# Linear attention and two feed-forward layers: the prices of the list schedule are changed

## The chip, the cores and the metric

The kernel runs on one core of a Trainium2 chip. The metric is the device time of one execution in microseconds (us). Three executions of the kernel before took 1591.6, 1592.91 and 1593.28 us; their median is 1592.91 us.

## What is computed

Inputs are q, k and v (8 batches, 8 heads, 576 positions, 64 values a head). Three steps follow each other, all in float32:

```python
kv = einsum('bhsd,bhse->bhde', k, v)             # attention without a softmax
out = einsum('bhsd,bhde->bhse', q, kv)
x = out / sqrt(mean(out*out) + 1e-6) * g_norm    # reordered to 4608 tokens x 512
x = (s * relu(x @ w_in1)**2 + b) @ w_out1        # 512 -> 2048 -> 512
h = x @ w_in2
y = (h * sigmoid(h)) @ w_out2                    # 512 -> 2048 -> 512
```

## The kernel before

The 4608 tokens are nine blocks of 512. TensorE multiplies in a 32-bit format with fewer mantissa bits, so each factor is held as a rounded part and a rest (`rnd` on ScalarE, line 214, and `rest` on VectorE or GpSimd, line 217), and one exact product is three matmuls of 512 columns: high by high, high by low, low by high (`mm3`, line 209). The kernel is bound by these.

The work has these stages.

1. **Attention of block 0**, in four pairs of heads (`attention_pair`, line 437, with `normalize`, line 565). A pair takes k, v and q from DRAM, multiplies k by v (`kv`, line 488: twenty small matmuls), copies that out of the bank (`kv_out`), turns q by a transposition on VectorE (`q_turn`, line 509), multiplies q by kv (`o`, line 518), multiplies the left-over 64 positions (`rem`, line 522, tile `r_ps`) and stores those (`orem`). While TensorE has nothing to do here, small warm-up matmuls fill it (line 1244).
2. **Seven plain blocks of layer 1** (`unit`, line 698). A unit is one block by 128 of the 2048 hidden columns: four exact products into bank `h` (`mm1`), then on ScalarE the relu, the square and the affine step (lines 730 to 737), the rounding (`g_hi`) and the rest (`g_lo`), and four exact products into the four banks `acc` (`mm2`). Sixteen units make a block. Beside the first block the weights of layer 1 are put together from a packed form (`decode`, line 275): load, three operations on ScalarE, three on VectorE and one on GpSimd for each weight tile. Four tiles come last, since room for them has to be made first (`turn`, line 1193): once all other tiles are done, the four come in halves through two load buffers `raw2`. Among them is the tile `wi15`, which unit 15 needs. Attention of the blocks 1 to 7 runs beside the units, and so does the making of factors for the next stage.
3. **Five stages on pairs of blocks** (`hidden`, line 923, and `outputs`, line 1060), one of layer 1 and four of layer 2, in which a two by two split of the matrices takes seven products for eight. Their results pass through three banks X, Y and Z and tiles `tmp`; ScalarE applies the curve (`curve`, `square`, `affine`, lines 997 to 1005).
4. **The last block of layer 2** as plain units again.

No engine's instruction order is written out by hand. Each operation is handed to a `Plan` (line 20) with the engine or engines that can do it and a price in us, a key (roughly the unit at which it is due), what it needs, what it makes, and which buffers it takes and gives back. `Plan.run` (line 45) walks a clock of its own: on each engine it looks for the operations that could start soonest by the prices so far, takes among those within 0.02 us the one with the lowest key, and emits it. So a price never changes an instruction; it changes when the planner believes things to be over, and with this in which order instructions stand in the queues of TensorE, ScalarE, VectorE, GpSimd and SyncE (which issues the loads and stores), and for some copies and rests which engine does them. Once emitted, each queue runs in its order. Warm-up matmuls carry the highest key and the limit `until=40`: the planner drops those that would begin after 40 us of its own clock.

The prices that matter here are those of the products (lines 543, 555, 720, 777, 954 and 1088), of the affine steps (lines 743 and 1012), and two functions of a width n for ScalarE, which give 0.525 and 0.622 us at 512 columns:

```python
    def act2(n):
        return {ACT: 0.11 + n * 1.0e-3}

    def act(n):
        return {ACT: 0.1 + n * 0.83e-3}
```

Of the kernel before, what the change touches and what calls it, by code (L numbers as in the profile page):

```python
# [19 lines left out]
class Plan:  # L20
# [19 lines left out]
    def add(self, engines, key, fn, needs=(), makes=(), takes=(), gives=(), move=None, opens=(), until=None):  # L40
        self.ops.append((key, len(self.ops), engines, fn, needs, makes, takes, gives, move, opens, until))
        for b in gives:
            self.users[b] = self.users.get(b, 0) + 1
# [89 lines left out]
def kernel(  # L133
# [30 lines left out]
    T = NCH * P  # L164
# [3 lines left out]
    LAG2 = 1.6  # L168
# [13 lines left out]
    def layer_of(tp):  # L182
        return 0 if tp < NL1 else 1
# [12 lines left out]
    tp = ctx.enter_context(tc.tile_pool(name="tp", bufs=1))  # L196
# [54 lines left out]
# [5 lines that stand above are left out]
# [181 lines left out]
    def attention_pair(bb, p, key, before=None):  # L437
# [99 lines left out]
        for i in range(P // Q):  # L537
# [2 lines left out]
        fr = (0, 0) if z else me  # L540

        prev, prev_r = ([], []) if z else ([("x32",) + before], [("ro",) + before])
        add({"PE": 0.8}, key, kv, needs=[f("k"), f("v"), ("kr",) + fr, ("vr",) + fr] + prev_r, makes=[f("kv")],
            takes=[b["psk"]], gives=[b["kv"], ("wo12", 0) if z else b["rem"]])
        add({ACT: 0.21, DVE: 0.26}, key + 0.3, kv_out, needs=[f("kv")] + ([("kvf0L",)] if z else []), makes=[f("kvf")],
            takes=[b["kvf"]], gives=[b["psk"]])
# [5 lines left out]
        add(act(T), key + 0.4, q_hi, needs=[f("qT")], makes=[f("qh")], takes=[b["qs"]], gives=[b["qT"]])  # L552
        add(both(T), key + 0.5, lambda e: rest(e, st["ql"], st["qT"][:, :T], st["qh"]), needs=[f("qh")], makes=[f("ql")],
            gives=[b["qT"]])
        add({"PE": 0.65}, key + 1.5, o, needs=[f("kvl"), f("ql"), f("kvh"), f("qh")] + prev,
            makes=[f("o")], takes=[b["pso"]], gives=[b["kvs"], b["qs"]])
        add({"PE": 0.2}, key + 2.2, rem, needs=[f("kvf"), f("qT")], makes=[f("r")], takes=[b["psr"]],
            gives=[b["kvf"], b["qT"]])
# [139 lines left out]
    def unit(u):  # L698
        layer, t, m = units[u]
        lb = LASTU if layer else t  # L700
        def ready(kind):
            if layer == 1:
                return [("w", 1, kind, m)]
            return [("w", 0, kind, m, c) for c in range(2 if (kind, m) in late else 1)]

        def w_gives(kind):
            if layer:
                return [("win" if kind == "i" else "wout", ("last", m))]
            return lent_to[f"w{kind}{m}"] if t == TP - 1 else []

        def mm1(kk):
            def go(e):
                if kk == 0:
                    h_t[u] = psum(("h", u), "h")
                w, f_ = w_t["i", layer, m], slice(kk * P, (kk + 1) * P)
                mm3(h_t[u], w[:, 0, f_], w[:, 1, f_], *xs[lb, kk], kk == 0, kk == KD - 1)
            return go

        for kk in range(KD):
            add({"PE": 0.648}, u + kk * 0.02, mm1(kk),  # L720
                needs=[("x", lb, kk)] + ready("i") + [("mm1o", u, kk - 1)] * (kk > 0) + ([("mm1o", u - 1, kk)] if u - 1 in units else []),
                makes=[("mm1", u, kk)], opens=[("mm1o", u, kk)], takes=[("h", u)] * (kk == 0),
                gives=([xs_of(lb, kk)] if lb != TP - 1 else [("ya", f"xh{kk}"), ("ya", f"xl{kk}")]) * (m == KF - 1) + w_gives("i"))


        gs = ("g2" if layer else "gh", u)
        if layer == 0 and u >= TP * KF - 3:
            plan.heir[gs] = "g2"

        def first(e):  # L730
            nc.scalar.activation(h_t[u], h_t[u], AF.Relu if layer == 0 else AF.Silu)  # L731

        def squares(e):
            nc.scalar.activation(h_t[u], h_t[u], AF.Square)

        def affine(e):
            nc.scalar.activation(h_t[u], h_t[u], AF.Identity, scale=s_t, bias=b_t)

        add(act(T), u + 0.1, first, needs=[("mm1", u, KD - 1)], makes=[("r", u)])
        src = ("r", u)  # L740
        if layer == 0:
            add(act(T), u + 0.2, squares, needs=[src], makes=[("sq", u)])
            add({ACT: 0.73}, u + 0.25, affine, needs=[("sq", u)], makes=[("aff", u)])
            src = ("aff", u)
        st = {}

        def g_hi(e):
            st["g"] = place2(gs)
            rnd(st["g"][0], h_t[u])

        def g_lo(e):
            rest(e, st["g"][1], h_t[u], st["g"][0])

        add(act(T), u + 0.3, g_hi, needs=[src], makes=[("gh", u)], takes=[gs])
        add({DVE: 0.69}, u + 0.35, g_lo, needs=[("gh", u)], makes=[("gl", u)], gives=[("h", u)])

        def mm2(d):
            def go(e):
                gh, gl = st["g"]
                w = w_t["o", layer, m]  # L760
                start, stop = m == 0, m == KF - 1
                if start:
                    a_t[d] = psum(("acc", (lb, d)), "acc")
                dd = slice(d * P, (d + 1) * P)
                if layer == 0:
                    mm3(a_t[d], w[:, 0, dd], w[:, 1, dd], gh, gl, start, stop)
                else:
                    nc.tensor.matmul(a_t[d], gh[:, dd], w[:, 0], start=start, stop=False)  # L768
                    nc.tensor.matmul(a_t[d], gh[:, dd], w[:, 1], start=False, stop=False)  # L769
                    nc.tensor.matmul(a_t[d], gl[:, dd], w[:, 0], start=False, stop=stop)  # L770
            return go

        for d in range(KD):
            acc = ("acc", (lb, d))
            if layer == 0 and t == TP - 1 and d == 0 and m == KF - 1:
                plan.heir[acc] = "h"
            add({"PE": 0.648}, u + LAG2 + d * 0.02, mm2(d),
                needs=[("gh", u), ("gl", u)] + ready("o") + [("mm2o", u - 1, d)] * (m > 0) + [("mm2o", u, d - 1)] * (d > 0)
                + [("omo", NPP - 1, NS // 2 - 1, 13)] * (layer == 1 and m == 0),
                makes=[("mm2", u, d)], opens=[("mm2o", u, d)], takes=[acc] * (m == 0), gives=[gs] + w_gives("o"))  # L780
            if m == KF - 1:
                block_out(layer, t, d, u + LAG2 + d * 0.02, acc)
        if layer:
            for kind in "io":
                b_ = ("win" if kind == "i" else "wout", ("last", m))

                def load(e, kind=kind, b_=b_):
                    tile_ = w_t[kind, 1, m] = place(b_)
                    for c in range(2):
                        dma(f32(tile_)[:, :, c * QW:(c + 1) * QW], w_d[1, kind, m // 2][:, quarter_of(kind, m % 2, c)])  # L790

                add({"SP": 0.96}, u - 5 + 0.1 * (kind == "o"), load, needs=[(b_[0] + "l", m - 1)] if m else [(b_[0] + "end",)],
                    makes=[("w", 1, kind, m)], opens=[(b_[0] + "l", m)], takes=[b_], move=1.46)
# [129 lines left out]
    def hidden(tp, j):  # L923
# [25 lines left out]
        for i in range(7):  # L949
            for kk in range(KH):  # L950
                before = [("hmo",) + me + (i, kk - 1)] if kk else [("hmo",) + me + (i - 1, KH - 1)] if i else (
                    [("hmo", tp, j - 1, 6, KH - 1)] if j else [("hmo", tp - 1, NS - 1, 6, KH - 1)] if tp else [("mm1o", TP * KF - 1, KD - 1)])
                first = BANK.index(BANK[i]) == i and kk == 0
                add({"PE": 0.68}, key + 4 / 7 * (i + 0.5 * kk), mm(i, kk),
                    needs=[("xo", i, tp, kk), ("wi", tp, j, i // 2)] + before + ([(read[i],) + me] if i in read and kk == 0 else []),
                    makes=[("hm",) + me + (i, kk)], opens=[("hmo",) + me + (i, kk)], takes=[bk[BANK[i]]] if first else [],
                    gives=[("win", (tp, j, i // 2))] + [(f"xo{i}{kk}", tp)] * (j == NS - 1))
# [37 lines left out]
        for src, ready, kk in (("d", done(3) + [("x1",) + me], k(3)), ("b", [("h22",) + me], k(4) + 0.1),  # L995
# [8 lines left out]
            def affine(e, src=src):  # L1004
                nc.scalar.activation(src_of(src), src_of(src), AF.Identity, scale=s_t, bias=b_t)

            sf = ("sg", src) + me
            add(act2(T), kk, curve, needs=ready, makes=[sf if layer_of(tp) else ("sr",) + sf], takes=[tb["d"]] if src == "d" else [],
                gives=[bk[X]] if src == "d" else [])
            if not layer_of(tp):  # L1010
                add(act2(T), kk + 0.01, square, needs=[("sr",) + sf], makes=[("sq",) + sf])
                add({ACT: 0.81}, kk + 0.02, affine, needs=[("sq",) + sf], makes=[sf])

        kt = k(6) + 0.2
        add({DVE: 0.69}, kt, add_up("e", B(Z), S("d"), ALU.subtract), needs=sg("a", "d"), makes=sg("e"), takes=[tb["e"]])
# [3 lines left out]
        for i, src, ready, kk, gives in (  # L1019
# [10 lines left out]
            def lo(e, src=src, i=i):  # L1030
                rest(e, g2[me, i][1], src_of(src), g2[me, i][0])

            add(act2(T), kk, hi, needs=ready, makes=[("gh",) + me + (i,)], takes=[gb])
            add({DVE: 0.69} if src in in_bank else {POOL: Port(1.3)}, kk + 0.03, lo, needs=[("gh",) + me + (i,)],
                makes=[("gl",) + me + (i,)], gives=gives)
        free = {bk[Z]: sg("f") + [("gl",) + me + (T3,)], tb["d"]: sg("f") + [("gl",) + me + (B11,)],
# [23 lines left out]
    def outputs(tp, q):  # L1060
# [3 lines left out]
        for n, (i, d) in enumerate(steps):  # L1064
# [14 lines left out]
            def total(e, i=i, d=d, st=st, ya=ya):  # L1079
# [5 lines left out]

            before = [("omo",) + me + (n - 1,)] if n else [("omo", tp, q - 1, len(steps) - 1)] if q else (
                [("omo", tp - 1, NG - 1, len(steps) - 1)] if tp else [("mm2o", TP * KF - 1, KD - 1)])
            add({"PE": 1.36}, key, mm,
                needs=[(x, tp, 2 * q + a, i) for x in ("gh", "gl") for a in range(2)] + [("wo", tp, q, i)] + before,
                makes=[("om",) + me + (i, d)], opens=[("omo",) + me + (n,)], takes=[acc],  # L1090
                gives=[("g2", (tp, 2 * q + a, i)) for a in range(2)] + [("wout", me + (i,))])
# [218 lines left out]
```

## Time and profile before

| what | us |
|---|---|
| median of three executions | 1592.91 |
| the profiled execution | 1593.07 |
| its span, first to last instruction | 1591.3 |
| TensorE busy | 1572.5 (99%) |
| VectorE busy | 1011.1 (64%) |
| ScalarE busy | 892.3 (56%) |
| GpSimd busy | 529.6 (33%) |

Engines in the rows: PE is TensorE's matmul, PEld its weight load, DVE is VectorE, ACT is ScalarE, POOL is GpSimd, SPq is SyncE's queue of transfers. A time "from the start" is counted from the first instruction of the span. In a row of the timeline, the two numbers are start and duration, and what stands in brackets is the engine's idle time before it and what ended that. Matmuls overlap, so one that takes 0.39 us follows the one before it sooner than that; what counts is from start to start. In a row by stretches, PEclk is the granted clock of TensorE as a share of its full 2.4 GHz.

### The profile page before, as it was taken

To read this page: it belongs to the slowest core of one execution; us is meant where nothing else is said; L and a number is where in the kernel's file an instruction comes from. 1 tells how busy PE (TensorE), PEld (TensorE's weight loads), DVE (VectorE), ACT (ScalarE), POOL (GpSimd) and SP (SyncE) were. 2 spreads that over 40 slices of the span, in tenths; PEclk is the share of its full clock that TensorE was granted. 3 is DMA by queue.
4 is the path that set the end of the run, shared out by engine and by line. 5 is a ranking of instruction groups with operands and counts; after the bars stand their busy time and mean duration, and the time that the engine had idled before them with its cause. 6 is when DMAs were issued, how large, how long until landed. Compare 5 with 4: busy or idle time off the path is not lost.

```text
span 1591.3 us, 23446 instructions
## 1 busy us (share of the span) xinstructions
PE 1572.5 (99%) x7500; PEld 1282.8 (81%) x7500; DVE 1011.1 (64%) x1890; ACT 892.3 (56%) x1719; POOL 529.6 (33%) x482
## 2 busy tenths in 40 slices
PE   8999999999999999999999999999999999999999
PEld 6877887878888888887888888888888888888887
DVE  6887777777667776535666656665667566656521
ACT  5997565666667776566767443544354445444222
POOL 1331111221122121131227652672276237622310
PEclk9999999999999999999999999999999999999999
DMA  8765867767667885797668786877688767876784
GB/s 213 197 177 152 260 213 228 228 195 223 197 200 229 237 244 180 260 346 234 192 192 265 237 272 194 285 202 231 190 288 197 237 196 261 199 237 188 211 210 132
DMA packets 377146, 351.30 MB, mean 221 GB/s; under 512 B 178240, under 2 KB 288832, under 8 KB 377024
## 3 DMA queue, kind: packets, MB, share of 16 engines
q1 hardware_dynamic: 376896, 349.81, 73.5%
q8 instruction: 60, 0.98, 0.3%
q14 instruction: 62, 0.51, 0.1%
q0 software_dynamic: 128, 0.00, 0.0%
HBM read 254.28 MB, written 95.42 MB: 220 GB/s over the span
## 4 chain that ended last, share of the span: by engine, by line
PE 92%; DMA 3%; SPq 2%; DVE 2%; ACT 1%; issue 1%; POOL 0%; DVEq 0%; ACTq 0%; POOLq 0%
PE hp L944 24%; PE acc L1075 8%; PE acc L1077 8%; PE acc L1076 8%; PE h L210 7%; PE h L211 7%; PE h L212 7%; PE acc L210 6%; PE acc L211 6%; PE acc L212 6%; SPq L227 2%; PE kv_ps L497 1%; DMA raw<-in_moe_w_out_dram 1%; PE acc L770 1%; PE acc L768 1%; PE acc L769 1%
## 5 line engine op out<-in xcount | busy, mean ns | idle before, releaser
L944 PE MATMUL hp<-xo,win 128*128 128x512 f32 x1680 | 427.5, 390 | 2.3 <-DVE tmp L969 2.0
L944 PEld LDWEIGHTS hp<-xo,win 128*128 128x128 f32 x1680 | 315.0, 188 | 72.0 <-DVE tmp L969 2.8
L218 POOL TENSOR_TENSOR g<-tmp,g 128x512 fp32r<-128x512 f32 x160 | 207.3, 1299 | 401.3 <-ACT g L215 305.8
L1084 DVE TENSOR_TENSOR ya<-acc,ya 128x512 f32<-128x512 f32 x210 | 145.0, 691 | 158.6 <-PE acc L1077 156.5
L1075 PE MATMUL acc<-g,wout 128*128 128x512 f32 x560 | 219.4, 392 | 0.0
L1077 PE MATMUL acc<-g,wout 128*128 128x512 f32 x560 | 218.9, 391 | 0.0
L1076 PE MATMUL acc<-g,wout 128*128 128x512 f32 x560 | 218.9, 391 | 0.0
L731 ACT ACTIVATE h<-h 128x512 f32<-128x512 f32 x128 | 74.5, 582 | 221.3 <-PE h L212 220.9
L210 PE MATMUL acc<-gh,wo 128*128 128x512 f32 x448 | 182.4, 407 | 1.6 <-DVE y L224 1.6
L210 PE MATMUL h<-xh,wi 128*128 128x512 f32 x448 | 177.3, 396 | 0.0
L211 PE MATMUL h<-xl,wi 128*128 128x512 f32 x448 | 176.1, 393 | 0.2 <-DVE xl L218 0.2
L212 PE MATMUL h<-xh,wi 128*128 128x512 f32 x448 | 176.0, 393 | 0.0
L211 PE MATMUL acc<-gh,wo 128*128 128x512 f32 x448 | 175.8, 392 | 0.1
L212 PE MATMUL acc<-gh,wo 128*128 128x512 f32 x448 | 175.6, 392 | 0.0
L323 POOL TENSOR_TENSOR rq<-raw 128x256 uint32<-128x256 uint32 x72 | 47.0, 654 | 253.4 <-DVE raw L309 117.0
L1077 PEld LDWEIGHTS acc<-g,wout 128*128 128x128 f32 x560 | 105.1, 188 | 23.4
L1076 PEld LDWEIGHTS acc<-g,wout 128*128 128x128 f32 x560 | 105.1, 188 | 22.5
L1075 PEld LDWEIGHTS acc<-g,wout 128*128 128x128 f32 x560 | 105.1, 188 | 22.5
L218 DVE TENSOR_TENSOR gh<-h,gh 128x512 fp32r<-128x512 f32 x112 | 76.7, 685 | 56.4 <-ACT gh L215 55.3
L215 ACT ACTIVATE g<-tmp 128x512 fp32r<-128x512 f32 x160 | 100.8, 630 | 14.6 <-DVE tmp L981 9.6
L969 DVE TENSOR_TENSOR tmp<-hp,tmp 128x512 f32<-128x512 f32 x120 | 82.4, 687 | 37.3 <-PE hp L944 32.9
L215 ACT ACTIVATE g<-hp 128x512 fp32r<-128x512 f32 x120 | 71.8, 598 | 58.3 <-PE acc L1077 22.3
(142 smaller groups left out, 2719.9 us busy)
## 6 DMA issues: line engine op xcount, KB each, us to landing
wout<-wo SPq DMA_DIRECT2D x312, 256.0 KB, 3.7
win<-wi SPq DMA_DIRECT2D x120, 512.0 KB, 4.8
wi<-rq SPq DMA_DIRECT2D x192, 128.0 KB, 2.2
wo<-rq SPq DMA_DIRECT2D x192, 128.0 KB, 2.6
win<-wi SPq DMA_DIRECT2D x72, 256.0 KB, 3.9
raw<-in_moe_w_out_dram SPq DMA_DIRECT2D x38, 256.0 KB, 3.5
raw<-in_moe_w_in_dram SPq DMA_DIRECT2D x34, 256.0 KB, 3.2
xt_d<-tmp SPq DMA_DIRECT2D x32, 256.0 KB, 5.6
```

The costliest lines, as they stand in the source:

```text
L210: nc.tensor.matmul(ps, wh, xh, start=first, stop=False)
L211: nc.tensor.matmul(ps, wh, xl, start=False, stop=False)
L212: nc.tensor.matmul(ps, wl, xh, start=False, stop=last)
L215: nc.scalar.activation(hi, src, AF.Copy)
L218: eng[e].tensor_tensor(lo, src, f32(hi), op=ALU.subtract)
L731: nc.scalar.activation(h_t[u], h_t[u], AF.Relu if layer == 0 else AF.Silu)
L944: nc.tensor.matmul(to, w[:, wn, f_], x_[:, xn], start=first and n == 0, stop=kk == KH - 1 and n == 2, skip_group_check=True)
L969: nc.vector.tensor_tensor(t, bank[me, a], tmp[b_, me], op=ALU.add)
L1075: nc.tensor.matmul(to, w[:, 0, dd], gh, start=a == 0, stop=False)
L1076: nc.tensor.matmul(to, w[:, 0, dd], gl, start=False, stop=False)
L1077: nc.tensor.matmul(to, w[:, 1, dd], gh, start=False, stop=a == 1)
L1084: nc.vector.tensor_tensor(y2[tp, i, d], st["ps"], y2[tp, i, d], op=ALU.add)
```

## The change

Prices only. The products of the plain blocks and of attention get the price that the pairs had nearly (0.648 or 0.65 to 0.682), those of the pairs move by 0.002 to 0.004, k times v goes from 0.8 to 0.97. On ScalarE the affine step of the plain blocks goes from 0.73 to 0.68; in the pairs the curve on a bank goes from `act2` to `act` (0.622 to 0.525), the square and the affine step on a bank go to 0.525 and 0.68, the affine step on a tile from 0.81 to 0.76, and every rounding `hi` of a result from `act2` to `act`. No instruction, buffer, key or dependency is touched.

```diff
-        add({"PE": 0.8}, key, kv, needs=[f("k"), f("v"), ("kr",) + fr, ("vr",) + fr] + prev_r, makes=[f("kv")],
+        add({"PE": 0.97}, key, kv, needs=[f("k"), f("v"), ("kr",) + fr, ("vr",) + fr] + prev_r, makes=[f("kv")],
...
-        add({"PE": 0.65}, key + 1.5, o, needs=[f("kvl"), f("ql"), f("kvh"), f("qh")] + prev,
+        add({"PE": 0.682}, key + 1.5, o, needs=[f("kvl"), f("ql"), f("kvh"), f("qh")] + prev,
...
-            add({"PE": 0.648}, u + kk * 0.02, mm1(kk),
+            add({"PE": 0.682}, u + kk * 0.02, mm1(kk),
...
-            add({ACT: 0.73}, u + 0.25, affine, needs=[("sq", u)], makes=[("aff", u)])
+            add({ACT: 0.68}, u + 0.25, affine, needs=[("sq", u)], makes=[("aff", u)])
...
-            add({"PE": 0.648}, u + LAG2 + d * 0.02, mm2(d),
+            add({"PE": 0.682}, u + LAG2 + d * 0.02, mm2(d),
...
-                add({"PE": 0.68}, key + 4 / 7 * (i + 0.5 * kk), mm(i, kk),
+                add({"PE": 0.682}, key + 4 / 7 * (i + 0.5 * kk), mm(i, kk),
...
-            add(act2(T), kk, curve, needs=ready, makes=[sf if layer_of(tp) else ("sr",) + sf], takes=[tb["d"]] if src == "d" else [],
+            price = act if src in in_bank or src == "d" else act2
+            add(price(T), kk, curve, needs=ready, makes=[sf if layer_of(tp) else ("sr",) + sf], takes=[tb["d"]] if src == "d" else [],
...
-                add(act2(T), kk + 0.01, square, needs=[("sr",) + sf], makes=[("sq",) + sf])
-                add({ACT: 0.81}, kk + 0.02, affine, needs=[("sq",) + sf], makes=[sf])
+                add((act if src in in_bank else act2)(T), kk + 0.01, square, needs=[("sr",) + sf], makes=[("sq",) + sf])
+                add({ACT: 0.68 if src in in_bank else 0.76}, kk + 0.02, affine, needs=[("sq",) + sf], makes=[sf])
...
-            add(act2(T), kk, hi, needs=ready, makes=[("gh",) + me + (i,)], takes=[gb])
+            add(act(T), kk, hi, needs=ready, makes=[("gh",) + me + (i,)], takes=[gb])
...
-            add({"PE": 1.36}, key, mm,
+            add({"PE": 1.364}, key, mm,
```

## Rows read from the trace of the kernel before

**Rows 1.** The page, part 1: busy us, share of the span, instructions.

```profile
PE 1572.5 (99%) x7500; PEld 1282.8 (81%) x7500; DVE 1011.1 (64%) x1890; ACT 892.3 (56%) x1719; POOL 529.6 (33%) x482
```

**Rows 2.** Stretches: length, busy us of each engine, PEclk, DMA share, GB/s.

```profile
0.00:47.80 47.80, 42.29 (x374) 32.39 (x375) 31.23 (x61) 28.04 (x65) 10.50 (x19) 1.00 0.90 216
47.80:104.80 57.00, 55.63 (x281) 45.08 (x279) 47.87 (x82) 53.30 (x104) 18.10 (x17) 1.00 0.73 199
104.80:108.20 3.40, 3.40 (x10) 2.68 (x9) 1.77 (x6) 3.40 (x7) 2.00 (x2) 0.53 0.72 195
108.20:138.90 30.70, 27.35 (x170) 21.69 (x168) 22.73 (x47) 23.16 (x52) 7.13 (x8) 1.00 0.47 127
138.90:145.70 6.80, 6.25 (x24) 4.67 (x26) 3.69 (x9) 3.43 (x9) 1.15 (x2) 0.51 0.97 209
145.70:640.00 494.30, 492.40 (x2519) 400.60 (x2514) 356.48 (x859) 332.39 (x725) 94.93 (x127) 1.00 0.73 216
...
735.00:760.00 25.00, 23.01 (x101) 18.32 (x100) 16.83 (x26) 20.54 (x36) 7.73 (x6) 1.00 0.60 188
760.00:1540.00 780.00, 779.66 (x3413) 640.32 (x3412) 484.49 (x742) 364.36 (x620) 368.39 (x289) 1.00 0.74 224
```

**Rows 3.** Waits of TensorE from 48 us on: total, times, longest.

```profile
PE r_ps L524 <- DVE qT L511: 2.7, 1, 2.7
PE hp L944 <- DVE tmp L969: 2.0, 2, 1.2
PE acc L210 <- DVE y L224: 1.6, 1, 1.6
PE r_ps L524 <- ACT kvf L222: 1.4, 1, 1.4
```

**Rows 4.** Timeline of TensorE, 116 to 143 us.

```profile
116.03 0.39 PE L210 MATMUL h<-xh,wi 128*128 128x512 f32 x1
...
116.71 0.39 PE L210 MATMUL acc<-gh,wo 128*128 128x512 f32 x1
...
117.48 0.69 PE L497 MATMUL kv_ps<-kv 128*64 128x64 f32 x16
...
118.35 0.50 PE L210 MATMUL acc<-gh,wo 128*128 128x512 f32 x1
...
139.45 0.66 PE L524 MATMUL r_ps<-qT,kvf 128*128 128x64 f32 x2 [2.73 <-DVE qT L511]
...
141.29 0.63 PE L210 MATMUL h<-xh,wi 128*128 128x512 f32 x1
...
142.57 0.63 PE L210 MATMUL h<-xh,wi 128*128 128x512 f32 x1
```

**Rows 5.** Timelines of SyncE, ScalarE and VectorE, 123 to 140 us.

```profile
123.09 0.83 SPq L227 DMA_DIRECT2D raw<-in_moe_w_out_dram  x2
...
130.66 0.38 SPq L227 DMA_DIRECT2D raw<-in_moe_w_in_dram  x1
...
137.22 0.42 ACT L215 ACTIVATE wi<-rq 128x256 fp32r<-128x256 f32 x1
...
138.52 0.78 DVE L511 STREAM_TRANSPOSE qT<-q 128x576 f32<-128x576 f32 x1 [1.40 <-DMA q<-in_q_dram]
139.22 0.38 DVE L218 TENSOR_TENSOR wi<-rq,wi 128x256 fp32r<-128x256 f32 x1
```

**Rows 6.** Timeline of ScalarE, 98 to 117 us.

```profile
98.07 0.70 ACT L300 ACTIVATE dw<-raw 128x512 f32<-128x512 f32 x1 [1.58 <-DMA raw<-in_moe_w_out_dram]
...
110.79 0.58 ACT L731 ACTIVATE h<-h 128x512 f32<-128x512 f32 x1 [1.01 <-PE h L212]
...
112.46 0.74 ACT L737 ACTIVATE h<-h,vecs 128x512 f32<-128x512 f32 x1
113.12 0.66 ACT L317 ACTIVATE raw<-raw 128x512 uint32<-128x512 uint32 x1
...
116.91 0.58 ACT L731 ACTIVATE h<-h 128x512 f32<-128x512 f32 x1 [0.53 <-PE h L212]
```

## The prediction

> **What bounds the kernel now.** I first read the busy times: TensorE is busy 1572.5 of 1591.3 us [rows 1], so no reordering can win more than what it idles, what it runs slowly, and what the start holds. Then the stretches [rows 2], where the reader is to see how unevenly that is spread. From 760 to 1540 us TensorE is idle for 0.34 of 780 us, in the pairs' stages therefore nothing can be won. From 145.7 to 640 us, six of the seven plain blocks, it is idle for 1.9 of 494.3 us. What there is lies in three places: the first 47.8 us (5.5 us idle, and warm-ups fill much of the rest), the first plain block up to 145.7 us, and the entry into the pairs at 735 to 760 us (2.0 us idle). The first plain block has idle times of 1.37, 3.35 and 0.55 us (lengths less busy times), and two stretches, 3.4 and 6.8 us long, at a granted clock of 0.53 and 0.51, the lower level of 1.2 GHz. The list of waits names the causes from 48 us on [rows 3]: the longest is 2.7 us of `r_ps` for the turned q, then 2.0 us of the pairs' first products for `tmp`, 1.6 us at a block's end for the copy of y, and 1.4 us of `r_ps` for the copy of kv. Each of the two waits of `r_ps` stands just ahead of one of the slow stretches; the other two, of about the same length as the shorter one, have none behind them.
>
> **The wait at 139 us.** In the timeline of TensorE [rows 4] a product of three matmuls takes 0.68 us (116.03 to 116.71), and `kv` 0.87 us (117.48 to 118.35). At 139.45 `r_ps` starts after 2.73 us of idling, and the next products need 1.28 us each (141.29 to 142.57). But `r_ps` isn't all that was late. The products behind it are those of unit 15, and their weight tile `wi15` was ready only when VectorE's rest of its second half, started at 139.22, had ended at 139.60 [rows 5]. That tile's history: the loads of the four last tiles start at 123.09, the second half of `wi15` is loaded only at 130.66, since two buffers serve all halves, ScalarE rounds it at 137.22 to 137.64, and VectorE gets to it at 139.22 because the transposition of q stands ahead of it in its queue and waits 1.40 us for its load. So two things end the wait at nearly the same time, and what moves both is when the last tiles begin, that is when the other 28 tiles are decoded.
>
> **Which engine the planner believes to be the limit there.** Per unit of the first block it counts for TensorE eight products, 5.18 us, and a quarter of a pair's attention (0.8 + 0.65 + 0.2 + 0.2 = 1.85), 0.46: 5.65 us. For ScalarE it counts relu, square and rounding at 0.525 and the affine step at 0.73, 2.31; two tiles of three operations at 0.525, 3.15; a quarter of a pair's 1.41 (two at 0.525, 0.2 and 0.16), 0.35: 5.81 us. With the new prices TensorE is 5.46 + 0.51 = 5.97 us and ScalarE 5.76 us. The planner's limit in this block thus passes from ScalarE to TensorE. The trace says that the new prices are nearer: 0.68 us for a product [rows 4], 0.66 us from the affine step to the next instruction (112.46 to 113.12) [rows 6]. The sign of the old error shows on ScalarE too. Twice it waits for the bank of a unit, 1.01 us before 110.79 and 0.53 us before 116.91 [rows 6], with decoding queued behind; the planner had believed the products done earlier than they were.
>
> **The change part by part.**
> - *First plain block.* With TensorE slower on the planner's clock, relu stands later in ScalarE's queue among the decoding, and those 1.54 us go to it. I let the last tiles begin 1.54 us sooner, so the 2.73 us wait shrinks to 1.2. What follows the waits: behind 1.6 and 1.2 us the clock stayed up, behind 1.4 it fell [rows 2, 3]. I take it as staying up. The second slow stretch does 6.25 us of work at half speed, so 3.1 us come back. Term: -4.6 us. Bounds: all idling and slow running of this block gone, -(1.37 + 1.7 + 3.35 + 0.55 + 3.1) = -10.1; on the other side one more such wait with its slow stretch, +2.7 + 3.1 = +5.8. I stay nearer the gain, since the two ScalarE waits are seen.
> - *What the decoding waits for instead.* The 1.58 us of ScalarE for a load before 98.07 [rows 6] are a transfer that landed late behind others on SyncE's queue. No price of a transfer changes, so I keep this, and the 1.4 us wait of `r_ps` with its 1.7 us of slow running; SyncE's queue is reordered along with the buffers that come free, so they can move either way, which the bounds above hold.
> - *Start.* `kv` at 0.97 spreads four pairs by 0.17 us each on the planner's clock only. TensorE is idle or warming there, waiting for loads and for ScalarE and VectorE, which cover it. Term 0; bounds -5.5 us (its idle time) to +2.7 us (the longest wait seen).
> - *The other plain blocks.* TensorE sets the pace on both planner's clocks, and the keys set the order. Other engines lose 0.034 us of hidden slack for each product. The stretch holds, beside the 1.6 us at a block's end, 0.3 us of waits; I take as much again, +0.3. Bounds: -1.9 (all gone) to +3.2 (the block's end wait at two more of the six ends). SyncE's and GpSimd's queues follow buffers that TensorE frees, so they shift with it.
> - *Pairs.* TensorE's prices move by 0.3%. ScalarE's cheaper curves and roundings change its order and which of ScalarE and VectorE copies an output; ScalarE is busy 364 of 780 us and VectorE 484 [rows 2], and this idle time is the cover. If the cover fails, a bank is read late and products wait as at the entry, 1.2 us at a time [rows 3]. Term 0, bounds -2.3 (the waits at the entry and the 0.34) to +2.4 (two more).
>
> Sum: -4.6 + 0.3 = -4.3 us against the profiled execution's 1593.07, its span and 1.8 us around it. That lies 0.16 above the median, so the forecast is 1592.91 - 4.3 = **1588.6 us**.
>
> **A rule weighed against these rows.** The clock term is 3.1 of the 4.3 us. The page "TensorE: Matmul & The Clock Gate" of the Trainium skill, in its Part 1, says that how many matmuls run slowly varies between runs of one kernel, and that the penalty is under 1% of a typical span and should not be fitted. The two slow stretches here cost 4.8 us, or 0.3%, which agrees with its size; by that rule the clock term falls out of the sum, which would be -1.5 + 0.3 = -1.2 us. I keep the term, because three executions within 1.7 us of each other leave little room for a stretch that comes and goes.
>
> **The rivals.** A difference of 0.2%, 3.2 us, is about what a measurement of this kernel can tell from none.
> - *The clock falls all the same.* The shortened wait of 1.2 us is followed by a slow stretch, as 1.4 us was at 103 us. Then only -1.2 us is left: 1591.7. For it: the row of 1.4 us. Against: 1.6 and 1.2 us without one. The rule of the page above would give the same time.
> - *The last tiles set the time themselves.* From 123.09 to 139.60 they take 16.5 us through two buffers, and ScalarE's 1.54 us may not be what moved the start. Then the wait stays and the change does nothing that shows: about 1593. For it: two loads in a row wait for a buffer. Against: the start at 123.09 follows the decoding.
> - *Everything in the first block fits.* If the planner's limit is now the true one, both waits of `r_ps` and both slow stretches go, -10 us: 1583. Against: late loads, which no price covers.
> - *Slower: a pair pulled ahead runs into its load.* Ahead of a gap the planner pulls attention of later blocks into TensorE's queue, and `r_ps` of such a pair waits for a q whose load came late. That is what happened at 139 us. The old, too low price of a product left other engines 5% more time than planned; the new one leaves none. One more such wait, decided as soon as a turned q is planned less than those 1.40 us of lateness ahead of its `r_ps`, costs 2.7 us and 3.1 us of slow running: 1598.7 if the gap at 139 us stays.
>
> **How the numbers follow.** Forecast 0.38 (own range 1585 to 1590), everything fits 0.09, clock falls 0.13, last tiles 0.14, slower 0.26. Faster by over 0.2% are the forecast and the fit, 0.47; within it the clock and the tiles, 0.27, less a little that small shifts at start and in the pairs carry over the line, 0.26; slower 0.27. The range leaves out a tenth on each side: down to 1581.5, the full gain and a little of the start's; up to 1598, nearly the whole slower case.
>
> **What would show it.** Right: ScalarE's waits for the bank before 117 us gone, the loads of the last tiles before 122 us, TensorE's wait near 139 us at about 1 us or less, and a single slow stretch in the first block; from 145.7 us on the same idle times as before. Wrong: a slow stretch of 6.8 us still there; first products of the plain blocks later than 47.8 us; a wait of over 2 us on `r_ps` elsewhere; more than 1 us of idling of TensorE between 760 and 1540 us.

## The result, and the profile after

The changed kernel takes 1602.74 us (median of six executions, 1601.04 to 1607.08) against 1592.88 us. The ratio is 1.0066 with a 95% interval of 1.0053 to 1.0079: slower by 0.66%, where 1588.6 us, faster by 0.27%, had been forecast. The profiled execution has a span of 1600.9 us, 9.6 us over the kernel before. One execution of a run further down (h2) took 1734.3 us at a granted clock of 0.85, and it is left out there.

The stretches of the changed kernel answer to [rows 2]; the columns are length, busy us of TensorE, its weight loads, VectorE, ScalarE and GpSimd, granted clock, DMA share and GB/s:

```profile
0.00:47.80 47.80, 42.53 (x365) 32.35 (x365) 31.29 (x62) 27.92 (x63) 10.53 (x19) 0.96 0.88 216
47.80:104.80 57.00, 56.34 (x281) 45.28 (x280) 47.00 (x85) 51.75 (x100) 18.96 (x18) 1.00 0.74 204
104.80:145.70 40.90, 38.20 (x227) 29.03 (x226) 31.21 (x67) 34.32 (x76) 10.45 (x12) 1.00 0.59 149
145.70:640.00 494.30, 489.74 (x2489) 397.07 (x2488) 356.94 (x858) 328.34 (x717) 92.42 (x125) 1.00 0.72 216
640.00:735.00 95.00, 91.90 (x398) 74.03 (x397) 37.08 (x53) 51.23 (x85) 18.49 (x14) 1.00 0.87 296
735.00:760.00 25.00, 20.97 (x83) 16.16 (x83) 11.82 (x18) 16.79 (x30) 6.44 (x5) 0.93 0.56 170
760.00:1540.00 780.00, 778.18 (x3406) 638.86 (x3405) 479.06 (x736) 372.68 (x635) 369.18 (x290) 1.00 0.74 224
```

The reader is to see three things. From 47.8 to 145.7 us the clock stays at its full level, and both slow stretches of the first block are gone. From 145.7 to 640 us TensorE idles for 4.6 us where it had idled for 1.9, and from 640 to 735 us for 3.1 where it had not idled at all. At the entry into the pairs it idles for 4.0 us instead of 2.0, and the clock falls there. Two smaller things stand in the same rows. The clock of 0.96 in the first 47.8 us is a stretch of 3.5 us at 0.51 from 12.4 us on, in the attention of block 0, which the kernel before doesn't have; unit 0 begins at 29.4 us all the same, where it had begun at 30.2. And from 760 to 1540 us TensorE idles for 1.8 us instead of 0.3. The longest waits of TensorE from 48 us on, beside [rows 3], tell who is late:

```profile
PE acc L211 <- DVE gh L218: 4.0, 7, 1.9
PE hp L944 <- DVE tmp L969: 4.0, 3, 2.9
PE m_ps L587 <- DVE orem L224: 2.8, 4, 1.0
PE hp L944 <- DMA win<-wi: 1.7, 2, 1.2
PE r_ps L524 <- DVE qT L511: 0.7, 1, 0.7
```

The `r_ps` wait of 2.7 us has become 0.7. In its place stand many short waits that the kernel before hardly had: for the rests `gh` of a unit, and of `m_ps` (the small matmul of the norm) for a copy of `orem`, both on VectorE. What became of the last tiles in the first block stands in the rows of SyncE, VectorE and TensorE, beside [rows 4] and [rows 5]:

```profile
122.42 0.82 SPq L227 DMA_DIRECT2D raw<-in_moe_w_out_dram  x2
...
128.00 1.40 SPq L227 DMA_DIRECT2D raw<-in_moe_w_in_dram  x2
...
135.73 0.42 DVE L218 TENSOR_TENSOR wi<-rq,wi 128x256 fp32r<-128x256 f32 x1
...
139.09 0.77 DVE L511 STREAM_TRANSPOSE qT<-q 128x576 f32<-128x576 f32 x1
...
140.01 0.41 PE L524 MATMUL r_ps<-qT,kvf 128*128 128x64 f32 x2 [0.71 <-DVE qT L511]
```

**One measure for all kernels.** TensorE's idle time leaves out slow issue, and attention moves between blocks from kernel to kernel. So I count as lost, up to a point of the trace, the time less the matmuls issued before that point at their pace: 0.2268 us for one of 512 columns (0.68 us for three, [rows 4]), 0.044 for one of the twenty of `kv`, 0.136 for one of `r_ps`, 0.1 for one of `m_ps`. All kernels issue the same numbers of these (6528, 640, 64, 72), so the losses of a kernel add up to its span less 1524.6 us. Warm-ups count as lost. Loss in us, from the profiled execution of each (one execution of four or more, which for one kernel lie up to 11 us apart; how much of that falls on a single column isn't known):

```
products' price, kernel      up to  units  units  unit 96 to  from   sum
                             u. 16  16-80  80-96  the pairs   there
0.648  before                 43.1    7.8    2.2     0.4      13.2   66.7
0.682  changed                38.0   12.5    2.0     5.1      18.7   76.3
0.615  f1                     41.6    8.0    2.1     1.0      19.9
0.647  h1                     38.0   10.0    7.2     0.6      22.2
0.649  h2                     40.7    7.5    6.3     1.5      15.9
0.648  e2, kv alone           38.2    7.2    6.0     1.0      15.0
0.648  e3, ScalarE alone      42.5   10.7    4.5    15.1      16.5
0.648  e4, all but products   41.9    9.9    3.5     0.6      13.9
0.648  f4, sums on GpSimd     40.4    7.8    3.0     3.1      17.7
0.648  g3, first block 0.682  40.7    8.6    2.7     1.1      15.7
0.682  e1, products alone     38.6   17.5    6.6     2.9      15.8
0.681  h3                     38.9   15.6    6.0     3.0      21.1
0.683  h4                     37.9   11.1    2.5     5.8      15.9
0.682  f3, sums on GpSimd     39.0   13.1    3.1     8.6      20.2
0.716  f2                     38.3   24.3    2.7     4.1      15.4
0.682  g1, longer lags        46.7    9.9    8.1     6.3      17.6
0.648  g2, longer lags        43.3   11.8    5.0     5.4      28.6
0.648  g4, later landing, kv  43.8    6.1    2.0     1.6      64.2
0.682  i1, later landing      39.5    6.5    1.4     3.0      52.5
0.648  i2, later landing, kv  39.5    5.6    2.0     0.9      62.9
```

The 9.6 us between the first two rows are thus -5.1 up to unit 16, +4.7 to unit 80, -0.2, +4.7 and +5.5. (The expectations quoted below use an earlier count, which differs by up to 0.4 us: 7.9 and 12.7 for 7.8 and 12.5, and 17.1 for 17.5.)

### The profile page after: what moved, and what is told of

The parts are those of the page before. It is cut to its first block, busy times and chain, and to the rows that moved or that the text cites. A ratio compares the mean times of both kernels' runs of the same rounds, so it can differ in the third digit from the quotient of the medians.

```text
span 1600.9 us, 23445 instructions
## 1 busy us (share of the span) xinstructions
PE 1574.9 (98%) x7489; PEld 1279.6 (80%) x7489; DVE 1001.3 (63%) x1884; ACT 897.2 (56%) x1725; POOL 526.5 (33%) x482
## 4 chain that ended last, share of the span: by engine, by line
PE 74%; DMA 10%; ACT 4%; DVE 4%; SPq 4%; issue 2%; POOL 2%; DVEq 0%; POOLq 0%; ACTq 0%
PE hp L944 22%; PE acc L1076 8%; PE acc L1078 7%; PE acc L1077 7%; PE h L210 4%; PE h L212 4%; PE h L211 4%; PE acc L210 4%; SPq L227 4%; PE acc L211 4%; PE acc L212 3%; DMA raw<-in_moe_w_out_dram 2%; DMA raw<-in_moe_w_in_dram 2%; DMA y<-y 1%; DMA wi<-rq 1%
## 5 line engine op out<-in xcount | busy, mean ns | idle before, releaser
L215 ACT ACTIVATE g<-tmp 128x512 fp32r<-128x512 f32 x160 | 100.8, 630 | 17.1 <-DVE tmp L981 12.3
L981 DVE TENSOR_TENSOR hp<-hp,tmp 128x512 f32<-128x512 f32 x120 | 83.3, 694 | 35.0 <-PE hp L944 34.6
```

What stands on the lines that cost most here:

```text
L215: nc.scalar.activation(hi, src, AF.Copy)
L981: nc.vector.tensor_tensor(t, a(), b_(), op=op)
```

## Experiments

Every run is timed in rounds beside the kernel before, whose medians there lie between 1589.8 and 1592.2 us. Two theories run through the expectations: *slack*, by which the too low price had left spare time, and a *new draw*, by which any change of prices gives another order and with it a few us either way.

**The parts alone.** e1 has only the products' lines of the diff, e2 only the line of `kv`, e3 only those of ScalarE, e4 all but the products':

```diff
 e1 -            add({"PE": 0.648}, u + kk * 0.02, mm1(kk),      (and mm2; o from 0.65)
 e1 +            add({"PE": 0.682}, u + kk * 0.02, mm1(kk),
 e2 -        add({"PE": 0.8}, key, kv,
 e2 +        add({"PE": 0.97}, key, kv,
```

> Only the three prices of the plain blocks' and attention's products are changed (0.648 and 0.65 to 0.682). Theory of slack (with a true price of a product, what waits for other engines is planned without the 5% of spare time that the old price left): this part carries the loss, 1599 to 1604 us. Theory of a new draw (any change of prices gives another order, and a few us either way that have nothing to do with which price was nearer): anything from 1588 to 1603 us, and the parts don't add up to the whole.

> Only the price of k times v is changed (0.8 to 0.97). Slack: under 1 us of difference, 1592 to 1594. New draw: another order from the first pair on, with 1588 to 1600 us.

> Only ScalarE's prices are changed (affine step of the plain blocks, and the pairs' curve, square, affine step and rounding). Slack: ScalarE's price of a plain unit falls by 0.05 of some 5.8 us, so nothing to lose in the plain blocks, 1592 to 1594; in the pairs the idle time of TensorE stays under 1 us. New draw: 1588 to 1600.

> All of the change but the three prices of the plain blocks' and attention's products, which stay at 0.648 and 0.65. Slack: the loss is gone, 1591 to 1595. New draw: the sum of e2 and e3 doesn't hold, and the time lies anywhere from 1588 to 1603.

Measured: e1 1606.03 us (ratio 1.0089, 1.0072 to 1.0106), e2 1594.87 (1.0027, 1.0015 to 1.0038), e3 1613.74 (1.0142, 1.0123 to 1.0160), e4 1599.33 (1.0049, 1.0033 to 1.0065). The parts don't add up: 14.6, 3.4 and 22.3 us by themselves, 10 together. All four lie outside what slack said; e2 and e4 lie within the new draw's ranges, e1 and e3 above both. e3, which slack had at 1592 to 1594, is the slowest of the four, and some 14 us of its loss are one event. In it the block of unit 96 gets its last attention pair so late that three waits follow each other (waits of TensorE, 640 to 735 us, and the stretch of 652 to 669 us):

```profile
PE acc L210 <- ACT gh L215: 4.9, 1, 4.9
PE h L210 <- ACT xh L215: 2.8, 1, 2.8
PE m_ps L587 <- DVE part L580: 1.5, 1, 1.5
```

```profile
652.30:669.40 17.10, 9.33 (x22) 6.77 (x22) 6.82 (x11) 8.23 (x15) 0.00 (x0) 0.50 0.43 142
```

Nothing there has a price that is wrong by microseconds; it is another order, and with the waits 17.1 us ran at the lower clock, in which TensorE was busy for 9.3. From unit 16 to unit 80, on the other hand, the column is orderly: 7.2 to 10.7 us at the old products' price, 17.5 at the new one alone and 12.5 in the changed kernel.

**The products' price as a dose.** f1 and f2 are the kernel before with the three prices at 0.615 and 0.716:

```diff
-            add({"PE": 0.648}, u + kk * 0.02, mm1(kk),
+            add({"PE": 0.615}, u + kk * 0.02, mm1(kk),      (f2: 0.716)
```

> The kernel before with the three prices of the plain blocks' and attention's products at 0.615 (5% under 0.648). Measure: what TensorE loses (time that isn't product, attention or known small matmuls) from unit 16 to unit 80, which is 7.9 us in the kernel before, 12.7 in the changed one and 17.1 with the products' price of 0.682 alone. Theory of slack: a still lower price leaves still more spare time, 5 to 8 us lost there, and under 0.5 us in all of waits of products for VectorE's rests. Theory of a new draw: no order by price, 7 to 17 us. The total can be anything from 1588 to 1605 us under both, since the stage's two ends are drawn anew.

> The kernel before with the same three prices at 0.716 (5% over the traced 0.682). Slack: more waits than at 0.682, 17 to 25 us lost from unit 16 to unit 80, 1605 to 1615 us in total. New draw: 7 to 17 us lost there, 1590 to 1605 us in total.

Measured: f1 1600.70 us (1.0059, 1.0041 to 1.0078), f2 1618.68 (1.0171, 1.0143 to 1.0199). f1 loses 8.0 us from unit 16 to unit 80 and f2 24.3, both as slack has it; f2's total lies over its range. Only f2 tells the theories apart, since 8.0 lies in both ranges, and f1 misses one point: a product waits 1.6 us for VectorE's rest `xl`, where under 0.5 us of such waits were expected. Over all kernels with unchanged lags and landings the column rises with the price from 0.648 on: 7.2 to 10.7 at 0.647 to 0.649, 11.1 to 17.5 at 0.681 to 0.683, 24.3 at 0.716. These don't overlap, though two of them are only 0.4 us apart; below 0.648 it doesn't fall any more (8.0 at 0.615). In f2 the same two waits are the longest (146 to 735 us; of the second, 1.6 us stand before unit 80):

```profile
PE m_ps L587 <- DVE orem L224: 7.0, 8, 1.8
PE acc L211 <- DVE gh L218: 4.9, 7, 1.2
```

The first of them goes with the price too: up to unit 80 `m_ps` waits for `orem` for 0 us in f1, 0.2 before, 2.8 in the changed kernel, 3.5 in e1 and 7.0 in f2. How a price of TensorE makes VectorE late is seen on ScalarE, from 146 to 540 us, in the kernel before, the changed one and f2:

```profile
ACT h L731 <- PE h L212: 89.6, 53, 3.7
...
ACT rq L300 <- DMA raw<-in_moe_w_in_dram: 2.9, 3, 1.4
```

```profile
ACT h L731 <- PE h L212: 74.4, 47, 3.6
...
ACT rq L300 <- DMA raw<-in_moe_w_out_dram: 9.2, 10, 2.5
ACT rq L300 <- DMA raw<-in_moe_w_in_dram: 7.8, 8, 1.8
```

```profile
ACT h L731 <- PE h L212: 51.0, 31, 3.8
...
ACT rq L300 <- DMA raw<-in_moe_w_in_dram: 11.6, 10, 2.3
```

All its waits for transfers in this stretch add up to 11 us in f1, 15 before, 29 in the changed kernel and 53 in f2. These are loads from the inputs (7, 6, 19 and 16 us) and stores whose buffer is to be written again (4, 9, 11 and 37 us): from the old price to the true one it is mainly the loads that grow, in f2 the stores. VectorE's waits for transfers don't follow the price as well: 25, 46, 49 and 51 us. With a low price the planner believes a unit's bank to be ready early, puts the relu ahead of the decoding, and ScalarE waits for TensorE, which costs nothing, while the transfers land. With the true price it puts the decoding first, and ScalarE waits for transfers with the units' own work queued behind, and VectorE waits for ScalarE or for a load of its own. The wait of 0.97 us at 458 us in the changed kernel shows it, on VectorE and then on TensorE:

```profile
456.81 0.30 DVE L319 TENSOR_SCALAR raw<-raw 128x256 uint32<-128x256 uint32 x1 [0.95 <-DMA raw<-in_moe_w_in_dram]
...
457.88 0.42 DVE L309 SCALAR_TENSOR_TENSOR raw<-rq,raw 128x256 uint32<-128x256 uint32 x1
458.21 0.22 DVE L224 COPY orem<-r_ps 128x64 f32<-128x64 f32 x1
```

```profile
456.43 0.33 PE L524 MATMUL r_ps<-qT,kvf 128*128 128x64 f32 x2
...
458.49 0.40 PE L587 MATMUL m_ps<-part,pairs_of 128*128 128x16 f32 x2 [0.97 <-DVE orem L224]
```

`r_ps` was over at 456.8, but its copy stands behind four decoding operations, the first of which waited 0.95 us for a load; `m_ps` has to wait for that copy, since both matmuls use the same two banks. (That late transfers are the cause of the whole column rests on this row, on the sums above and on the landing runs below; the other waits were not traced one by one.)

**The sums on GpSimd.** In the changed kernel, from 640 to 735 us, the subtractions of the pairs' sums wait for loads on VectorE with `gh` behind them. f3 and f4 give them to GpSimd alone, in the changed kernel and in the one before:

```diff
-            add(both(T), key + 0.5 + 0.01 * m, go, needs=needs, makes=[("sx", o) + me])
+            add({POOL: Port(1.3)}, key + 0.5 + 0.01 * m, go, needs=needs, makes=[("sx", o) + me])
```

> The changed kernel with the subtractions for the pairs' sums (line 870) on GpSimd alone. In the changed kernel they wait for late loads in VectorE's queue with the plain units' rests behind them, and units 96 to 111 lose 4.9 us (0.3 in the kernel before). If that queue is the cause: the loss there falls to under 1.5 us, 1597 to 1600 us in total. If it is not: no change there, 1601 to 1604 us. Rival: GpSimd, with 1.3 us for each, makes the sums later and the entry into the pairs waits longer, over 1604 us.

> The kernel before with the same subtractions on GpSimd alone. It loses only 0.3 us in those units, so there is nothing to win there: 1591 to 1593 us by the theory of VectorE's queue. New draw: another order around the entry into the pairs, 1589 to 1598 us.

Measured: f3 1608.26 us (1.0101, 1.0081 to 1.0122), f4 1597.87 (1.0045, 1.0029 to 1.0061). A miss: with that queue cleared, f3 loses 8.6 us from unit 96 to the pairs instead of 5.1, now by 4.6 us in two waits of products for ScalarE's `gh`; its time is the rival's (over 1604 us), but at the entry and behind it loses only 1.5 us more than the changed kernel, so the rival's reason isn't shown. f4, for which that theory had 1591 to 1593 us, lies at the upper edge of the new draw. What ends the plain stage isn't one queue.

**Longer lags.** g1 (changed) and g2 (before) add 0.25 us to what the planner allows behind each operation of ScalarE, VectorE and GpSimd:

```diff
-    LAG = {"PE": 0.2, "ACT": 0.15, "DVE": 0.13, "POOL": 0.15}
+    LAG = {"PE": 0.2, "ACT": 0.4, "DVE": 0.38, "POOL": 0.4}
```

> The changed kernel, true prices of products kept, with 0.25 us more in the planner's lag behind each operation of ScalarE, VectorE and GpSimd (0.15, 0.13, 0.15 to 0.40, 0.38, 0.40). Theory of slack: spare time is what was lost, wherever it is put in, so the loss from unit 16 to unit 80 falls from 12.7 to 7 to 9 us, and the waits for the copy of orem and for the rests gh from 6.6 to under 2 us. Rival, the ratio of prices: the order that goes with 0.648 matters and not the spare time; then the loss stays at 11 to 15 us. Total under slack 1590 to 1600 us.

> The kernel before with the same longer lags. Slack: there is spare time enough, so 6 to 8 us lost from unit 16 to unit 80 (7.9 before). In the first block ScalarE and VectorE set the pace, and longer lags put the planner's order further from the true one there: 40 to 46 us lost up to unit 16 (43.2 before). Total 1588 to 1600 us.

Measured: g1 1610.75 us (1.0112, 1.0081 to 1.0143), g2 1620.68 (1.0174, 1.0159 to 1.0189). g1 loses 9.9 us from unit 16 to unit 80, between the two theories' ranges, and `m_ps` waits for `orem` for 0.2 us only; but up to unit 16 it loses 46.7. g2 loses 11.8 where slack had 6 to 8. Both totals lie far over slack's. Spare time behind every operation alike isn't the cure.

**True prices in the first block only** (g3), with `kv` at 0.97:

```diff
+            add({"PE": 0.682 if u < KF else 0.648}, u + kk * 0.02, mm1(kk),      (and mm2)
```

> True prices only where TensorE's price set the planner's limit: 0.682 for the products of the first block's 16 units, 0.97 for k times v, and 0.648 from unit 16 on, ScalarE's prices as before. Slack together with the prediction's reading of the first block: 37 to 39 us lost up to unit 16 (43.2 before, 38.0 in the changed kernel) and 6 to 9 us from there to unit 80; 1586 to 1595 us, by what the entry into the pairs gives. If the first block's gain and the later loss can't be had apart: over 12 us lost from unit 16 to 80, or over 41 up to unit 16.

Measured: 1596.34 us (1.0027, 1.0016 to 1.0039). From unit 16 to unit 80 it loses 8.6 us, as expected; up to unit 16 40.7, half of the gain looked for. The total lies over the range, by that half and by the ends.

**Later landing.** g4 has `kv` at 0.97 and lets the planner's transfers land 1.5 us later:

```diff
-    DMA_START, DMA_END = 0.7, 1.1
+    DMA_START, DMA_END = 0.7, 2.6
```

> Only the price of k times v at 0.97, and the planner's landing of a transfer 1.5 us later (1.1 to 2.6), nearer to the landings seen (2.2 to 6 us medians). If the ends of the plain stage lose by transfers planned too early: from unit 96 to the first product of the pairs under 1.5 us lost, and waits of the pairs' first products under 2 us; 1584 to 1592 us. Rival, the two ends are drawn anew by any change: 1588 to 1605 us.

Measured: 1645.31 us (1.0332, 1.0315 to 1.0350), and yet the smallest loss from unit 16 to the pairs (9.7 us) of the kernels up to then. The total is a miss: far more is given back at the entry into the pairs, where waits of under 2 us were expected of the first products (735 us to the end):

```profile
PE hp L944 <- ACT tmp L222: 23.8, 1, 23.8
PE hp L944 <- ACT xo L215: 7.2, 1, 7.2
PE hp L944 <- DVE tmp L969: 7.0, 3, 4.7
```

So i1 (changed) and i2 (`kv` alone) allow the later landing in the plain stage behind its first block only:

```diff
-                end = dma + self.DMA_END
+                end = dma + (2.6 if 11 < op[0] < 90 else self.DMA_END)
```

> The changed kernel, where the planner takes a load or store with a key between 11 and 90 (the plain stage after its first block) to land 1.5 us later (2.6 for 1.1). Theory of late loads: with the true price of a product, ScalarE's and VectorE's operations on loaded data stand further ahead in their queues and wait there for loads, in front of the units' own; from 146 to 540 us ScalarE waits 15 us for loads in the kernel before, 29 in the changed one, 53 at a price of 0.716. Then this edit brings that back to under 15 us and the loss from unit 16 to unit 80 from 12.5 to 6 to 8.5 us, with the first block's 38 us kept. Rival, the spare time of the whole chain and not of loads: 11 us or more still lost. Total by the ends' draw, 1593 to 1605 us.

> Only k times v at 0.97, products at 0.648, and the same later landing for keys between 11 and 90. Late loads: up to unit 16 as with k times v alone (38 us lost), 5.5 to 7 us from unit 16 to unit 80; with ends like those seen (2.6 to 8 us from unit 80 to the pairs' first product, 13 to 22 from there to the end) 1586 to 1600 us. It would be the fastest so far if its ends are drawn as in the kernel before.

Measured: i1 1631.09 us (1.0251, 1.0226 to 1.0276), i2 1639.59 (1.0305, 1.0279 to 1.0331). In the stage that they were made for both do what late loads foretold: 6.5 and 5.6 us lost from unit 16 to unit 80, ScalarE's waits for transfers from 146 to 540 us down to 3.6 and 3.3 us, the first block's gain nearly kept (39.5). The edit moves loads and stores alike, so it doesn't tell which of the two was late; and it shows that the true price of the products can stay where the planned landing is longer (i1). The pairs' first product stands at 721.2 and 718.6 us, against 728.3 in the changed kernel and 724.2 before. But the entry breaks again, in i1 by one wait (540 us to the end):

```profile
PE hp L944 <- DVE tmp L969: 38.2, 3, 36.4
...
```

Ahead of it ScalarE waits 26.3 us for the store of a sum before it can reuse the `tmp` tile:

```profile
ACT tmp L999 <- DMA xt_d<-tmp: 26.3, 1, 26.3
```

The totals expected of both are missed. An order that keeps the 6 us and enters the pairs as the kernel before does wasn't found; no version beats the kernel before.

**A price moved by 0.15%.** What was still open was whether the ends of the stage have anything to do with the new values. h1 and h2 are the kernel before at 0.647 and 0.649 (attention's product, at 0.65, goes to the same price), h3 and h4 the changed one at 0.681 and 0.683:

```diff
-            add({"PE": 0.648}, u + kk * 0.02, mm1(kk),
+            add({"PE": 0.647}, u + kk * 0.02, mm1(kk),      (h2: 0.649; h3, h4: 0.681 and 0.683 for 0.682)
```

> The kernel before with the products' price of the plain blocks and attention at 0.647 instead of 0.648 (attention's from 0.65). A change of 0.15% says nothing of which price is nearer. If the losses outside units 16 to 80 (the start and first block, the plain stage's last units, the entry into the pairs, the pairs' loads) come from the new values: within 1 us of the kernel before, about 1592. If they are a new draw of the order: 1588 to 1605 us. In both cases 7 to 10 us lost from unit 16 to unit 80, by the price.

> The same at 0.649. New values: about 1592 us. New draw: 1588 to 1605 us. 7 to 10 us lost from unit 16 to unit 80.

> The changed kernel with the same price at 0.681 instead of 0.682. New values: about 1602 us. New draw: 1592 to 1615 us. In both cases 12 to 17 us lost from unit 16 to unit 80, by the price.

> The changed kernel at 0.683. New values: about 1602 us. New draw: 1592 to 1615 us. 12 to 17 us lost from unit 16 to unit 80.

Measured: h1 1602.44 us (1.0069, 1.0054 to 1.0084), h2 1599.19 (1.0045, 1.0033 to 1.0057), h3 1608.41 (1.0104, 1.0087 to 1.0120), h4 1602.61 (1.0068, 1.0051 to 1.0086). One thousandth of a microsecond on the products' price (three on attention's in h1) makes the kernel before 10.7 and 7.4 us slower, as much as the whole change; new values would have left it within 1 us. The changed kernel becomes 5.7 us slower at 0.681 and stays as it was at 0.683. From unit 16 to unit 80 h1, h2 and h3 lose what their price foretold, and h4 loses 11.1 us where 12 to 17 were expected: for a thousandth that column moves by some 3 us, the ends by up to 14. From unit 80 to the end the kernel before loses 15.8 us (2.2 + 0.4 + 13.2); every other kernel of the table loses 18 or more there, the changed one 25.8, h1 30.0, h2 23.7. The kernel before is the best draw of its ends among twenty; the changed one is in the middle.

## Why the prediction was wrong

- **The first plain block was right in its sign and in what was to shrink, and its size is in part luck.** The term was -4.6 us; the loss up to unit 16 fell by 5.1. The waits of `r_ps` went from 2.7 and 1.4 us to 0.7 and less, ScalarE's waits for a bank from 98 to 118 us are gone, and the clock held. By the same count the 5.1 are 0.6 gained up to unit 0, 1.7 lost up to unit 8, and 6.1 gained from there on, where the first slow stretch and its wait went as well, which the term had kept. How it came about was only half seen: the last tiles' loads begin at 122.42 instead of 123.09 us, 0.67 us sooner and not 1.54. But the halves of `wi15` are now loaded together at 128.00 us, where the second had left at 130.66, and VectorE makes the second's rest at 135.73 instead of 139.22, ahead of the turn of `q` and not behind it. Five kernels at 0.681 to 0.683 lose 37.9 to 39.0 us there, the seven wholly at 0.647 to 0.649 38.0 to 43.1, so the old price could draw this gain too.
- **The rule on the clock.** The term for the slow stretches, kept against it, came back with the waits, and the changed kernel paid another one at the entry: after the wait of 2.92 us a stretch of 3.50 us has a granted clock of 0.52. In these traces the lower level comes behind waits, though not behind each. The advice not to fit it, in the Trainium skill's "TensorE: Matmul & The Clock Gate" (Part 1), is given there for the ramp at a kernel's start; taken over to stretches inside the span, as I had done in weighing it, it would have left out 4.8 us that the first block got back.
- **"Other engines lose 0.034 us of hidden slack for each product ... +0.3"** is the first step that failed. It measured +4.7 us from unit 16 to unit 80, beyond its own bound of +3.2. The step took slack per product and saw no wait that it could open. In its place the runs show ScalarE waiting for transfers for 29 us instead of 15, and 2.8 us of `m_ps` behind VectorE's queue instead of 0.2. My reading, which no run shows by itself, is that a transfer is planned many products ahead of its use, so that the 5% adds up over that whole distance; the kernel before had its spare time in ScalarE's 90 us of waiting for TensorE, in a stretch whose idle time I read as a sign that nothing depended on it.
- **The terms of 0 behind unit 80** are the second, and the larger: +4.7 us before the pairs (the row from 640 to 735 us wasn't read at all; the +0.3 was worked out from 145.7 to 640) and +5.5 us from there on, where 0, with -2.3 to +2.4, was set. The entry's waits went from 2.0 to 4.0 us with a slow stretch, the loads `win` from 0.34 to 1.7; the prediction had named over 1 us of idling from 760 to 1540 us as a sign of being wrong, and it was 1.8. I costed reordering at nothing where the kernel before shows no idle time; the 0.15% runs show that these ends move by 2 to 14 us under a reordering that no new value asks for. That a dense stage stays dense was the unspoken assumption. Which operation makes a given order late there stays open.
- **The rival on the slower side** had the sign and named one wait of 2.7 us behind a late q. From 48 us on there was no such wait of `r_ps`; there were many short ones of others, and its time of 1598.7 was 4 us too low. The rival that everything in the first block fits came true in its place (no slow stretch, waits of 0.7 us and under), though with a gain of 5.1 us and not 10, and not in the total.
- **Net**: up to unit 80 the changed kernel is 0.4 us faster than the one before; the whole of the 9.6 us lies behind it.

## What to carry to other kernels

Where a planner writes the order, a price that is too low for the busiest engine can be a margin for the others, as it was here from unit 16 to unit 80; setting it true needs that margin put back where it was used, here in the landing of transfers. (A price lower still, 0.615, gave no more of it.) Before crediting or blaming such a change, move a price by a thousandth: if the time scatters as much as the change did, the change can't be told from the draw. And a stage without idle time isn't safe from a reordering: its density belongs to the order that it has.

## What was not expected of the hardware

A wait of a few microseconds can cost about as much again by the clock. In the kernel before, 1.4 us were followed by 3.4 us at 0.53 (1.7 us more by half speed) and 2.7 us by 6.8 us at 0.51 (3.1 more) [rows 2, 3]. In the changed kernel a single wait of 2.92 us was followed by 3.5 us at 0.52, in which TensorE was busy for 3.3 (1.7 more). In e3 the waits of 1.5, 2.8 and 4.9 us came with 17.1 us at 0.50, busy for 9.3 (4.7 more). The length of a wait doesn't decide it alone: behind 1.6 us in the kernel before, and 1.9 us in the changed one, the clock stayed up. The two slow stretches of the changed kernel as rows:

```profile
12.40:15.90 3.50, 3.50 (x24) 2.29 (x21) 1.20 (x2) 1.46 (x5) 0.00 (x0) 0.51 0.99 217
...
743.00:746.50 3.50, 3.32 (x8) 2.67 (x9) 1.17 (x3) 1.40 (x3) 1.28 (x1) 0.52 0.21 78
```
